# Loading 8 KB of gate weights in one transfer instead of four, with the spreading moved to VectorE

## The chip, the cores and the metric

The kernel runs on one core of one Trainium2 chip. The metric is the device time of one execution in microseconds (us), lower is better. An execution counts as slow when it takes over 1.5% longer than the fastest of the same kernel, and only fast ones are compared. Times below are medians of a kernel's runs; the span that a profile shows is about 1.75 us shorter than the time. Runs of one kernel scatter by some 0.3 us either way, and the effect studied here is about 0.4 us.

## The reference

Four batches of cross-covariance attention (6400 x 256) feed a mixture of eight low-rank adapters, of which the gate picks two for each row.

```python
def _attn_ref(q, k, v, tau):                       # each (4, 6400, 256)
    qn = q / (np.linalg.norm(q, axis=1, keepdims=True) + 1e-06)
    kn = k / (np.linalg.norm(k, axis=1, keepdims=True) + 1e-06)
    s = kn.transpose(0, 2, 1) @ qn / tau           # 256 x 256 per batch
    s = s - s.max(-1, keepdims=True)
    a = np.exp(s)
    a /= a.sum(-1, keepdims=True) + 1e-09
    return (v @ a).astype(np.float32)

def _moe_ref(x, w_gate, A, B):                     # x (25600, 256), w_gate (256, 8)
    logits = x @ w_gate
    # ... the two best of eight experts for each row, softmax of their two logits ...
    # delta = sum over the two of w * ((x @ A[e]) @ B[e])
    return (x + delta).astype(np.float32)
```

## The kernel before

The kernel is a static schedule: a small simulator in the file plans every step, and the instructions are issued in that order. The parts here are the loads of the small weights, the copies that bring them to bf16, and the stores, which all go through the Sync queue.

```python
    def load_consts():                       # after the second load is issued
        first = W["first"].rearrange("p c d -> p (c d)")
        W["A0"] = first[0:P // 4, 4 * C:8 * C].rearrange("p (e g r) -> p e g r", e=E, r=R)
        nc.sync.dma_start(W["A0"], moe_A.rearrange("e (p g) r -> p e g r", g=8))
        W["B0"] = first[:, 8 * C:9 * C]
        nc.scalar.dma_start(W["B0"], moe_B.rearrange("e r d -> (e r) d"))
        W["wg0"] = first[:, 9 * C:9 * C + CC * E].rearrange("p (cc e) -> p cc e", e=E)
        wg = moe_w_gate.rearrange("(p g cc) e -> g p cc e", g=4, cc=CC)
        for g in range(4):
            nc.scalar.dma_start(W["wg0"][g * (P // 4):(g + 1) * (P // 4)], wg[g])
    # ...
    def do_wts(s):                           # VectorE, near 34.5 us
        W["A"] = const.tile([P, E, CC, R], BF16, name="a_raw")
        for g in range(4):
            nc.vector.tensor_copy(W["A"][g * (P // 4):(g + 1) * (P // 4)], W["A0"][:, :, CC * g:CC * g + CC, :])
        W["wg"] = const.tile([P, CC, E], BF16, name="wg_raw")
        nc.vector.tensor_copy(W["wg"], W["wg0"])
        W["B"] = const.tile([P, C], BF16, name="ball")
        nc.vector.tensor_scalar(out=W["B"], in0=W["B0"], scalar1=0.5, scalar2=None, op0=OP.mult)
    # ...
    def do_hold(s, kind, b, i):              # three of them: hold the stores back until a load of k has landed
        # ...
        nc.sync.dma_start(scrap, src)
    # ...
    def do_store(s, b, i, c, n):             # 24 of them, the last six within 10 us
        lo = i * PC + c
        nc.sync.dma_start(out_v[b, :, lo:lo + n, :], held["y", (b, i), ""][:, c:c + n, :])
```

## Time and profile before

| | before |
|---|---|
| time, median (lowest to highest) | 256.07 us (255.68 to 256.32), 3 runs |
| span of the profile | 254.4 us |
| busy: TensorE, VectorE, ScalarE | 85%, 75%, 66% of the span |
| read and written in HBM | 78.91 + 26.21 MB, 413 GB/s over the span |

First, the page's parts on engines and transfers: busy time of each engine, then packets and bytes, then the queues with packets, MB and the share of 16 engines' time that their packets took. The queue q10 is the one that the Activation engine issues on, q1 belongs to the Sync engine, q0 to GpSimd.

```profile
PE 217.1 (85%) x2641; PEld 193.2 (76%) x2643; DVE 189.6 (75%) x483; ACT 166.7 (66%) x270; POOL 30.0 (12%) x58
...
DMA packets 11964, 66.47 MB, mean 261 GB/s; under 512 B 1568, under 2 KB 2464, under 8 KB 7328
...
q0 software_dynamic: 7488, 39.06, 74.7%
q1 hardware_dynamic: 3968, 26.61, 25.7%
q10 hardware_dynamic: 480, 0.40, 0.7%
```

Shares of 74.7 and 25.7% already exceed 100: packets overlap on an engine. By this measure the engines have no free time, but it counts recorded packet times. The table by stretches says the same (start and end, length, busy time of each engine, granted TensorE clock, share of the transfer engines, GB/s):

```profile
4.00:46.00 42.00, 23.91 (x197) 18.14 (x198) 22.28 (x34) 20.73 (x19) 6.94 (x14) 0.94 1.06 216
48.00:68.00 20.00, 19.64 (x262) 17.79 (x260) 16.71 (x43) 14.36 (x27) 3.49 (x5) 0.92 1.04 217
68.00:88.00 20.00, 20.00 (x253) 18.74 (x252) 17.77 (x38) 14.63 (x21) 2.13 (x4) 1.00 1.03 239
128.00:158.00 30.00, 30.00 (x377) 27.95 (x378) 24.97 (x52) 21.98 (x36) 2.22 (x5) 1.00 1.04 217
206.00:230.00 24.00, 23.20 (x331) 21.15 (x328) 19.64 (x58) 16.83 (x32) 0.53 (x1) 1.00 1.02 350
```

TensorE is full in some stretches and half idle up to 46 us. By this measure the transfers are full in all of these (1.02 to 1.06). Next, the timeline of VectorE around the weight copies and around its one gap (start, duration, instruction, and in brackets the idle time before it with its cause):

```profile
35.67 0.17 DVE L525 CAST wg_raw<-y 128x16 bf16<-128x16 f32 x1
35.75 0.29 DVE L527 TENSOR_SCALAR ball<-y 128x256 bf16<-128x256 f32 x1
...
43.09 0.43 DVE L595 TENSOR_TENSOR ssqq<-ssq 128x256 f32<-128x256 f32 x1
43.84 1.76 DVE L586 TENSOR_TENSOR ssq<-ssq,sq 128x1536 f32<-128x1536 f32 x1 [0.33 <-ACT sq L580]
```

Then the timeline of ScalarE's queue at the start. The four issues take 2.02 us, and ScalarE's own work begins after them:

```profile
1.66 2.02 ACTq L483 DMA_DIRECT2D y<-in_moe_w_gate_dram  x4
3.70 1.28 ACT L497 ACT_TABLE_LOAD   x1 [3.70 <-issue]
5.00 0.20 ACT L497 ACTIVATE scrap<-neg_inv_tau 1x1 bf16<-1x1 f32 x1
5.11 1.12 ACT L738 CAST qk<-y 128x512 bf16<-128x512 f32 x2
```

### The profile page before, as it was taken

The page shows a single profiled execution, that of the slowest core. Times are in us where ns is not written, and L with a number is a line of the kernel's source. Part 1 is how long each engine was busy: PE and PEld are TensorE (multiplying, and loading weights), DVE is VectorE, ACT ScalarE, POOL GpSimd, SP SyncE. Part 2 cuts the span into 40 slices and gives each one's busy share as a digit, 9 for nine tenths or more (in the row PEclk, how much of TensorE's full clock was granted, in tenths as well). Part 3 has the DMA queues.
Part 4 walks back from the last instruction along what each step waited for, and adds up shares of the span by engine and source line. Part 5 has one row for each costly group of instructions (what it writes and reads, how often), then busy time and mean ns, then how long its engine had stood idle before and what let it go on. Part 6 is the DMA issues. An engine that isn't in the chain of part 4 may idle for free.

```text
span 254.4 us, 6345 instructions
## 1 busy us (share of the span) xinstructions
PE 217.1 (85%) x2641; PEld 193.2 (76%) x2643; DVE 189.6 (75%) x483; ACT 166.7 (66%) x270; POOL 30.0 (12%) x58
## 2 busy tenths in 40 slices
PE   0165984899999998999989999889999979999970
PEld 0053962598999996799789998779999759999860
DVE  0055589779889977898979995689888878888910
ACT  3344446558786766888768667543777859768770
POOL 7000220040020002000130100510000200000000
PEclk9999997599999999999999999999999999999995
DMA  8999999999999999999999999999999999999994
GB/s 188 215 218 208 211 220 213 213 220 215 213 218 210 317 293 293 259 216 219 210 215 220 214 216 216 214 208 353 276 287 320 337 315 315 321 426 422 423 411 174
DMA packets 11964, 66.47 MB, mean 261 GB/s; under 512 B 1568, under 2 KB 2464, under 8 KB 7328
## 3 DMA queue, kind: packets, MB, share of 16 engines
q0 software_dynamic: 7488, 39.06, 74.7%
q1 hardware_dynamic: 3968, 26.61, 25.7%
q10 hardware_dynamic: 480, 0.40, 0.7%
q8 instruction: 20, 0.33, 0.5%
q14 instruction: 8, 0.07, 0.1%
HBM read 78.91 MB, written 26.21 MB: 413 GB/s over the span
## 4 chain that ended last, share of the span: by engine, by line
PE 54%; DMA 34%; DVE 3%; ACT 3%; POOL 2%; issue 1%; DVEq 0%; ACTq 0%; POOLq 0%
DMA qk<-in_k_dram 28%; PE Y_ps L877 13%; PE Y_ps L881 7%; PE T_ps L753 7%; DMA v<-in_v_dram 6%; PE ZL_ps L775 5%; PE gzT_ps L864 3%; PE acc_417 L558 2%; PE acc_418 L558 2%; PE acc_2620 L558 2%; PE acc_2621 L558 2%; PE Z_ps L844 2%; DVE a_bf L727 2%; POOL qk L543 1%; PE log_ps L790 1%
## 5 line engine op out<-in xcount | busy, mean ns | idle before, releaser
L586 DVE TENSOR_TENSOR ssq<-ssq,sq 128x1280 f32<-128x1280 f32 (+1 forms) x27 | 43.4, 1607 | 26.7 <-ACT sq L580 24.7
L877 PE MATMUL Y_ps<-a_bf,vT 128*128 128x256 bf16 x400 | 60.0, 273 | 0.0
L580 ACT ACTIVATE sq<-qk 128x1280 f32<-128x1280 bf16 (+1 forms) x27 | 36.8, 1364 | 25.9 <-DVE ssq L586 19.3
L733 ACT COPY y<-Y_ps 128x512 f32<-128x512 f32 x79 | 45.8, 587 | 12.2 <-PE Y_ps L881 9.6
L558 PEld LDWEIGHTS <-qk 128*128 128x128 bf16 x400 | 33.8, 103 | 24.9 <-DMA qk<-in_k_dram 15.3
L733 ACT COPY vT<-T_ps 128x1024 bf16<-128x1024 bf16 (+1 forms) x44 | 37.0, 871 | 7.7 <-PE T_ps L753 7.5
L877 PEld LDWEIGHTS <-vT 128*128 128x128 bf16 x400 | 37.6, 98 | 3.7
L881 PE MATMUL Y_ps<-ball,gzT 128*128 128x256 bf16 x200 | 38.2, 273 | 0.3 <-DVE gzT L735 0.3
L558 PE MATMUL acc_110<-qk 128*128 128x256 bf16 x50 | 15.0, 310 | 16.9 <-DMA qk<-in_k_dram 10.6
L753 PE MATMUL T_ps<-ident,v 128*128 128x128 bf16 x400 | 28.0, 224 | 0.6 <-DMA v<-in_v_dram 0.6
L543 POOL DMA_DIRECT2D v<-in_v_dram x20 | 12.2, 612 | 128.7 <-PE T_ps L753 81.5
L562 PEld LDWEIGHTS <-qk 128*128 128x128 bf16 x242 | 24.3, 100 | 3.4
L753 PEld LDWEIGHTS <-v 128*128 128x128 bf16 x400 | 24.6, 100 | 1.9 <-DMA v<-in_v_dram 1.5
L881 PEld LDWEIGHTS <-gzT 128*128 128x128 bf16 x200 | 19.4, 98 | 3.0 <-DVE gzT L735 0.6
L775 PE MATMUL ZL_ps<-waA_sb,vT 128*128 128x136 bf16 x280 | 19.6, 222 | 1.1 <-DVE waA_sb L721 0.9
L864 PE MATMUL gzT_ps<-ident,gz 128*128 128x128 bf16 x200 | 19.7, 219 | 0.3
L775 PEld LDWEIGHTS <-vT 128*128 128x128 bf16 x280 | 17.7, 98 | 1.8 <-issue 1.3
L735 DVE COPY gzT<-gzT_ps 128x512 bf16<-128x512 bf16 (+1 forms) x39 | 15.0, 390 | 5.5 <-PE gzT_ps L864 4.8
L580 ACT ACTIVATE ssq<-qk 128x1536 f32<-128x1536 bf16 x8 | 11.9, 1483 | 10.2 <-DMA qk<-in_q_dram 4.8
L735 DVE COPY y<-Y_ps 128x512 f32<-128x512 f32 x21 | 14.3, 690 | 3.3 <-PE Y_ps L881 3.3
L733 ACT COPY zl<-ZL_ps 128x272 f32<-128x272 f32 (+1 forms) x35 | 14.0, 447 | 3.1 <-PE ZL_ps L775 3.0
L567 PEld LDWEIGHTS <-qk 128*128 128x128 bf16 x168 | 14.8, 98 | 1.2 <-issue 0.2
(304 smaller groups left out, 440.9 us busy)
## 6 DMA issues: line engine op xcount, KB each, us to landing
out_dram<-y SPq DMA_DIRECT2D x18, 1280.0 KB, 17.8
v<-in_v_dram POOLq DMA_DIRECT2D x20, 640.0 KB, 20.3
qk<-in_q_dram POOLq DMA_DIRECT2D x7, 1088.0 KB, 24.0
qk<-in_k_dram POOLq DMA_DIRECT2D x7, 1088.0 KB, 28.9
qk<-in_q_dram POOLq DMA_DIRECT2D x2, 1024.0 KB, 18.5
qk<-in_k_dram POOLq DMA_DIRECT2D x2, 1024.0 KB, 22.8
out_dram<-y SPq DMA_DIRECT2D x4, 512.0 KB, 6.6
qk<-in_q_dram POOLq DMA_DIRECT2D x2, 512.0 KB, 17.4
```

What stands on the lines that cost most here:

```text
L558: nc.tensor.matmul(acc[ic][:, 0:256], kt[:, j, ic * P:(ic + 1) * P], qt[:, j, :], start=c == 0, stop=False, skip_group_check=True)
L562: nc.tensor.matmul(acc[ic][:, 256:384], kt[:, j, ic * P:(ic + 1) * P], kt[:, j, ic * P:(ic + 1) * P], start=False, stop=False, skip_group_ ...
L567: nc.tensor.matmul(acc[ic][:, 384:512], qt[:, j, ic * P:(ic + 1) * P], qt[:, j, ic * P:(ic + 1) * P], start=False, stop=c == NC - 1, skip_ ...
L580: nc.scalar.activation(out[:, 0:n, :], t[:, j:j + n, :], ACT.Square)
L586: nc.vector.tensor_tensor(out=t, in0=t, in1=held["sq", (w, b, g), ""][:, 0:n, :], op=OP.add)
L733: nc.scalar.copy(out, in_)
L735: nc.vector.tensor_copy(out, in_)
L753: nc.tensor.matmul(ps[:, ic, j, :], vt[:, c + j, ic * P:(ic + 1) * P], W["ident"], is_transpose=True, start=(ic + j == 0), stop=(ic == CC ...
L775: nc.tensor.matmul(ps[:, j, :], vT[:, ic, c + j, :], st[b]["waA"][:, ic, :], start=(j == 0 and ic == 0), stop=(j == n - 1 and ic == CC - 1 ...
L864: nc.tensor.matmul(ps[:, j, :], gz[:, j, :], W["ident"], is_transpose=True, start=(j == 0), stop=(j == n - 1))
L877: nc.tensor.matmul(ps[:, j, :], vT[:, ic, c + j, :], st[b]["a"][:, ic, :], start=(j == 0 and ic == 0), stop=False, skip_group_check=True)
L881: nc.tensor.matmul(ps[:, j, :], gzT[:, c + j - UNITS[u][0], :], W["B"], start=False, stop=(j == 1), skip_group_check=True)
```

## The change

The gate weights are 256 x 8 floats, 8 KB. The kernel before loads them with four transfers of 32 rows of 64 bytes, one into each group of 32 partitions. The change loads them with one transfer of 32 rows of 256 bytes into the first 32 partitions, and VectorE, which has to make a bf16 copy anyway, writes that copy to the four groups in four instructions. The intent is to save three transfers.

```diff
-        W["wg0"] = first[:, 9 * C:9 * C + CC * E].rearrange("p (cc e) -> p cc e", e=E)
-        wg = moe_w_gate.rearrange("(p g cc) e -> g p cc e", g=4, cc=CC)
-        for g in range(4):
-            nc.scalar.dma_start(W["wg0"][g * (P // 4):(g + 1) * (P // 4)], wg[g])
+        W["wg0"] = first[0:P // 4, 9 * C:9 * C + 4 * CC * E].rearrange("p (g cc e) -> p g cc e", g=4, e=E)
+        nc.scalar.dma_start(W["wg0"], moe_w_gate.rearrange("(p g cc) e -> p g cc e", g=4, cc=CC))
@@ do_wts
-        nc.vector.tensor_copy(W["wg"], W["wg0"])
+        for g in range(4):
+            nc.vector.tensor_copy(W["wg"][g * (P // 4):(g + 1) * (P // 4)], W["wg0"][:, g])
```

## The prediction

> **What bounds the kernel now.** The transfer engines never rest: the table by stretches puts the DMA share at 0.99 to 1.10 from 4 to 230 us. TensorE shares the limit: busy 19.64 of 20 us from 48 to 68 us, 20.00 of 20 from 68 to 88. The chain of waits runs through transfers of k from 3.51 to 46.07 us, then mostly through TensorE, and again through transfers from 128.6 to 157.6 and 191.7 to 205.7 us.
>
> **What the change does.** The instruction order stays the same on every engine but for two places: the Activation queue issues one gate-weight transfer instead of four, and VectorE makes four copies 32x16 instead of one 128x16.
>
> 1. Issuing. The four issues take 2.02 us (1.66 to 3.68 us); one takes about 0.49. ScalarE's table load (now at 3.70 us) should start near 2.2 us. The first casts (5.11 us) gain at most 0.1 us: the first k block lands at 5.04 us. The chain gains nothing: after four matmuls from 6.28 us TensorE waits for k data until 14.77 us.
>
> 2. Transfers. The Trainium skill (DMA: Bandwidth & Descriptors, "Why a DMA increments its semaphore by 16 and not by 1") says that each participating engine ends its share of a transfer with a semaphore write. The trace agrees: the Activation queue's 480 packets are 384 of data (128 each for k, B, gate weights) + 6 x 16. So 96 data and 48 semaphore packets go: 336 remain. Cost, an estimate: that queue took 0.7% of 16 engines' 254.4 us = 28.5 us. At the store queue's rate (26.61 MB in 25.7%: 25.4 KB per us and engine) its 0.40 MB takes 15.8 us; the other 12.7 us over 224 to 480 packets is 26 to 57 ns each. 144 packets are 3.8 to 8.2 us, or 0.2 to 0.5 us on each of 16 engines, while the chain is the k transfers. Shares above 1 mean packets overlap, so perhaps half becomes time.
>
> 3. VectorE. The one copy takes 174 ns and the next instruction begins 80 ns after it. Three more should cost 0.25 to 0.5 us at 35.7 us. VectorE is busy without a break from 32.8 to 43.5 us, then waits 0.33 us for a ScalarE square whose start a q transfer set. That gap takes most of the delay. The rest (0 to 0.2 us) can reach rqI, which ends at 47.63 us, while TensorE takes it up at 48.01 us: 0.4 us more slack.
>
> **On the critical path:** -0.1 to -0.4 us from transfers, 0 to +0.2 us from VectorE.
>
> **Prediction:** 255.8 us, 8 in 10 between 254.9 and 256.6. Faster by over 2%: 0.01; within 2%: 0.98; slower: 0.01.
>
> **What would show it.** Gate issues fall from four to one, the Activation queue's packets to 336; the table load starts near 2.2 us; TensorE's restart (14.77 us) comes 0 to 0.4 us earlier; four copies in a row near 35.6 us total 0.4 to 0.7 us; VectorE's gap at 43.8 us shrinks; the rq_ps matmul at 48.23 us moves by under 0.4 us; later stages keep their lengths.
>
> **What would make it wrong.** Small packets holding up the shared engines far longer than their own time (then over 1 us faster); a clock step that moves a whole window; or later loads and stores meeting differently, which could move the end by 1 us either way.

## More of the kernel before

The program gives each transfer issued from the Sync and Activation queues one of eight completion semaphores, in turn. (Such a semaphore is a counter by which a transfer tells that its data has landed, so that an engine can wait for it.)

Last, the end of the program on the Sync queue. The first line comes from the view of waits (total us, times, longest). The others list the Sync queue's instructions of the closing line after 252.7 us (count, shortest, median and longest duration in ns, first and last start):

```profile
SPq L940 <- DMA out_dram<-y: 5.7, 3, 3.9
...
L940 SPq EVENT_SEMAPHORE  x8: 17/28/28, 253.2 to 254.3; - x8
L940 SPq DRAIN  x3: 7/7/7, 253.5 to 253.8; - x3
```

The view of the output tensor gives the last two stores with their first and last start, and the time from issue to landing:

```profile
L889 SPq DMA_DIRECT2D out_dram<-y x2: 332/332/333, 246.3 to 246.9; - x2
...
DMA to landing us min/median/max: 6.2/6.2/6.2
```

So the last store is issued at 246.9 us and lands near 253.1 us (253.15 by the trace's time stamps).

## The result and the profile after

| | before | after |
|---|---|---|
| median of 5 runs | 256.10 us (255.68 to 256.32) | 255.84 us (255.37 to 255.88) |
| span of the profile | 254.4 us | 254.1 us |
| packets of the Activation queue | 480 | 336 |
| last store landed at | 253.15 us | 253.14 us |
| span's end minus last landing | 1.215 us | 0.908 us |

The ratio of the two is 0.998, with a 95% interval of 0.9968 to 0.9992. Ratios here are the mean time of one kernel's fast runs over that of the other's of the same rounds, so not quite the ratio of the quoted medians. The changed kernel is faster by 0.2%, and the interval excludes a ratio of 1.

The last two rows of the table come from the trace's time stamps and surprise. The data was all out at the same moment in both executions. The 0.31 us between the two spans lies after it.

Here are the lines of the profile after. Transfers, from the page:

```profile
DMA packets 11820, 66.47 MB, mean 262 GB/s; under 512 B 1424, under 2 KB 2320, under 8 KB 7184
...
q10 hardware_dynamic: 336, 0.40, 0.6%
```

VectorE's timeline at the same two places. The copies and the instruction after them take 0.65 us more (36.34 - 35.61 = 0.73 us from the first copy to the next instruction, against 0.08 us), and the gap before the sum at 44 us is gone; that sum starts 0.18 us later than before:

```profile
35.61 0.70 DVE L524 CAST wg_raw<-y 32x16 bf16<-32x16 f32 x4
36.34 0.29 DVE L526 TENSOR_SCALAR ball<-y 128x256 bf16<-128x256 f32 x1
...
43.68 0.42 DVE L594 TENSOR_TENSOR ssqq<-ssq 128x256 f32<-128x256 f32 x1
44.02 1.75 DVE L585 TENSOR_TENSOR ssq<-ssq,sq 128x1536 f32<-128x1536 f32 x1
```

ScalarE's timeline at the start, with everything earlier than before:

```profile
1.66 0.46 ACTq L481 DMA_DIRECT2D y<-in_moe_w_gate_dram  x1
2.15 1.28 ACT L495 ACT_TABLE_LOAD   x1 [2.15 <-issue]
...
4.62 1.14 ACT L737 CAST qk<-y 128x512 bf16<-128x512 f32 x2 [0.97 <-DMA y<-in_q_dram]
```

And the end on the Sync queue, the wait line and the instructions after 252.7 us:

```profile
SPq L939 <- DMA out_dram<-y: 5.9, 6, 1.2
...
L939 SPq EVENT_SEMAPHORE  x3: 17/17/28, 253.2 to 254.0; - x3
L939 SPq DRAIN  x3: 7/7/7, 253.2 to 253.5; - x3
```

with the last store, from the view of the output tensor:

```profile
L888 SPq DMA_DIRECT2D out_dram<-y x1: 332/332/332, 246.5 to 246.5; - x1
...
DMA to landing us min/median/max: 6.6/6.6/6.6
```

It was issued 0.4 us earlier and took 0.4 us longer, so it landed when it did before. The transfer engines still had earlier stores to work off: their share is 0.93 from 246 to 250 us and 0.39 from 250 to 252.5 us (before, 0.95 and 0.39).

Read the closing lines against the same lines of before. After the last landing the Sync queue has eight semaphore instructions to run before, and three after. The waits on stores tell why. Before, the closing part stops three times for a store, the first time for 3.9 us; after, it stops six times, at most 1.2 us. The closing part checks the eight completion semaphores one by one in a fixed order (each check is one instruction, which also names a second semaphore). In the kernel before, the last six stores use the semaphores 5, 6, 7, 0, 1, 2 (counted from 0), so the last store's is the third to be checked, and five checks that have long been satisfied are still to come when it lands. In the trace these follow one another every 61 ns on average. Three transfers less shift the assignment by three: the last six stores now use 2 to 7, the last store's semaphore is the eighth and last, and no check is left. Five times 61 ns is 0.31 us.

The Trainium skill (Perfetto Trace Analysis, "Identifying Dependency Chains") says that an instruction that waits for several engines may have EventSemaphore instructions with further wait conditions put in front of it. The trace agrees: these lines are EVENT_SEMAPHORE instructions with two wait conditions each, in front of a DRAIN. It adds their price, 61 ns each even when there is nothing to wait for.

### The profile page after: what moved, and what is told of

It is laid out like the page before. It is cut to its first block, busy times and chain, and to the rows that moved or that the text cites. A ratio compares the mean times of both kernels' runs of the same rounds, so it can differ in the third digit from the quotient of the medians.

```text
span 254.1 us, 6344 instructions
## 1 busy us (share of the span) xinstructions
PE 216.1 (85%) x2643; PEld 192.7 (76%) x2643; DVE 190.0 (75%) x486; ACT 166.8 (66%) x270; POOL 30.1 (12%) x58
## 4 chain that ended last, share of the span: by engine, by line
PE 49%; DMA 39%; ACT 3%; DVE 3%; POOL 2%; issue 1%; ACTq 0%; POOLq 0%
DMA qk<-in_k_dram 22%; PE Y_ps L876 13%; DMA v<-in_v_dram 9%; DMA qk<-in_q_dram 8%; PE Y_ps L880 6%; PE T_ps L752 6%; PE ZL_ps L774 4%; PE gzT_ps L863 3%; PE Z_ps L843 2%; PE acc_417 L557 2%; PE acc_418 L557 2%; DVE a_bf L726 2%; PE acc_2620 L557 1%; PE acc_2621 L557 1%; ACT a_exp L678 1%
## 5 line engine op out<-in xcount | busy, mean ns | idle before, releaser
L752 PE MATMUL T_ps<-ident,v 128*128 128x128 bf16 x400 | 27.1, 220 | 0.3 <-DMA v<-in_v_dram 0.3
L752 PEld LDWEIGHTS <-v 128*128 128x128 bf16 x400 | 23.9, 98 | 1.5 <-DMA v<-in_v_dram 1.2
```

The source lines that it names most:

```text
L752: nc.tensor.matmul(ps[:, ic, j, :], vt[:, c + j, ic * P:(ic + 1) * P], W["ident"], is_transpose=True, start=(ic + j == 0), stop=(ic == CC ...
```

## The experiments

Two theories compete for the 0.4 us. The theory says that removed transfer work at the start makes everything end earlier. The rival, found in the traces after the first set of runs, says that the last store's semaphore moved to a better place in the closing checks. There are two more suspects, VectorE's longer copying and ScalarE's earlier start. Each kernel was run for five rounds beside the kernel before; in a set, all share the same runs of the kernel before (set one: median 256.19 us; set two: 256.01 us; set three: 256.05 us). Set one ran on one chip (numbered 4), sets two and three on another (12). Where a kernel had four or six runs, it is said.

### Set one: parts of the change

**The change again.** No edit.

> The changed kernel again, unaltered, as the anchor of this set. If the 0.2% of the first measurement is real, the ratio to before is again 0.997 to 0.999 (0.3 to 0.8 us faster). If the first measurement was luck or only a property of that chip, it is 0.999 to 1.001.

Measured: 255.63 us, ratio 0.9982 (0.9970 to 0.9995). The gain is real and repeats in another set of runs. End minus last landing was 0.90 us again.

**The copies alone.**

```diff
 (kernel before)
-        nc.vector.tensor_copy(W["wg"], W["wg0"])
+        for g in range(4):
+            nc.vector.tensor_copy(W["wg"][g * (P // 4):(g + 1) * (P // 4)], W["wg0"][g * (P // 4):(g + 1) * (P // 4)])
```

> The kernel before, with only VectorE's part of the change: four gate transfers as before, but four copies of 32x16 instead of one of 128x16. Result right. My theory: VectorE is 0.5 to 0.6 us later from 36.3 us on, the 0.33 us gap at 43.8 us takes it, and rq_ps does not start over 0.2 us later; ratio 0.9995 to 1.0010. Rival (the copies reach the end in full, and the transfers save twice what the result shows): +0.5 us, ratio 1.002.

Measured: 256.01 us, ratio 1.0000 (0.9986 to 1.0014). VectorE's part costs nothing at the end that these runs can see; the interval allows 0.36 us either way. The trace shows where it goes. This is VectorE's timeline of this kernel:

```profile
35.74 0.76 DVE L526 CAST wg_raw<-y 32x16 bf16<-32x16 f32 x4
36.53 0.29 DVE L528 TENSOR_SCALAR ball<-y 128x256 bf16<-128x256 f32 x1
...
43.87 0.43 DVE L596 TENSOR_TENSOR ssqq<-ssq 128x256 f32<-128x256 f32 x1
44.21 1.75 DVE L587 TENSOR_TENSOR ssq<-ssq,sq 128x1536 f32<-128x1536 f32 x1
```

The instruction after the copies starts 0.78 us later than before (36.53 against 35.75), more than the expected 0.5 to 0.6; the matmul rq_ps, the next step on TensorE, is not later (48.15 against 48.23). The sum after the gap starts 0.37 us later than before (44.21 against 43.84). In this execution the attention matrix of the first batch (a_bf) came 0.78 us later than before (54.91 against 54.13 us), and yet the last store landed at 252.90 us, 0.25 us earlier than in the profile of before. In this one execution a delay of the compute engines was swallowed later, while the transfers ran on.

**The single transfer alone, with one copy.** The result is wrong (relative error 0.027), because the copy takes other rows.

```diff
 (changed kernel)
-        for g in range(4):
-            nc.vector.tensor_copy(W["wg"][g * (P // 4):(g + 1) * (P // 4)], W["wg0"][:, g])
+        nc.vector.tensor_copy(W["wg"], W["B0"][:, 0:CC * E].rearrange("p (cc e) -> p cc e", e=E))
```

> The changed kernel with its single gate transfer but one copy of 128x16 as before, taken from the other weights' rows, so gate values and result are wrong on purpose[...]. My theory (the gain is all from the three transfers less, the copies cost nothing at the end): the same ratio as the changed kernel, 0.997 to 0.999. Rival (the copies cost 0.5 us): 0.5 us faster than the changed kernel, ratio about 0.996.

Measured: 255.53 us, ratio 0.9981 (0.9968 to 0.9994), the same as the whole change. So the gain belongs to the transfers, not to the copies. This run cannot say whether it is their work or their number, since the semaphores shift along with them.

**Four transfers from the idle Sync queue.**

```diff
 (kernel before)
-            nc.scalar.dma_start(W["wg0"][g * (P // 4):(g + 1) * (P // 4)], wg[g])
+            nc.sync.dma_start(W["wg0"][g * (P // 4):(g + 1) * (P // 4)], wg[g])
```

> The kernel before with its four gate transfers issued from the idle Sync queue: all packets and semaphore writes stay, only ScalarE is free 2 us earlier (table load near 1.7 us). Result right. My theory (engine time of packets): no gain, ratio 0.9993 to 1.0007, and TensorE's first matmul, though up to 0.5 us earlier, changes nothing later. Rival (the gain is ScalarE's earlier start): ratio as the changed kernel's, about 0.998.

Measured: 256.11 us, ratio 0.9998 (0.9986 to 1.0011). ScalarE's earlier start (its table load at 1.67 us) is worth nothing that shows.

So far everything agrees with the theory. Then the time stamps of the six traces were laid side by side. End minus last landing was 1.215, 1.215 and 1.207 us in the three kernels with four gate transfers, and 0.908, 0.899 and 0.899 us in the three with one. The last landings were 253.15, 252.90 and 253.40 us against 253.14, 252.96 and 253.13 us. The first pair of triples does not overlap and hardly scatters; the second overlaps. That is where the rival came from.

### Set two: the order of the closing checks, without the transfers

The hold step of the kernel already issues transfers of 32 bytes on the Sync queue. These kernels issue some more of 4 bytes, at the first hold near 79 us, only to turn the assignment of semaphores. The hold's own transfer is cut to four elements to make room in the scratch tile. The tiny transfers are not quite free: with five of them the first store is issued at 82.69 us instead of 79.51.

```diff
-        nc.sync.dma_start(scrap, src)               # src has 16 elements
+        nc.sync.dma_start(scrap[:, 0:4], src)       # src cut to 4 elements
+        if "tiny" not in W:
+            W["tiny"] = 5                           # 5 in the kernel before; 3 or 1 in the changed kernel
+            for n in range(W["tiny"]):
+                nc.sync.dma_start(scrap[:, 4 + 2 * n:6 + 2 * n], src[:, 0:2])
```

**Kernel before plus five tiny transfers** (last store on the eighth semaphore):

> The kernel before (four gate transfers, one copy) with five transfers of 4 bytes added on the Sync queue near 79 us, so that the last store's completion semaphore is the eighth of the eight, as in the changed kernel, and not the third. Result right. New theory (most of the gain sits after the last landing: the closing waits of the Sync queue go through the eight semaphores in order, about 61 ns each, and five of them follow the last store's in the kernel before): end minus last landing falls from 1.21 to 0.90 us, ratio 0.9985 to 0.9995. Rival, my theory on record (the gain is all removed transfer work at the start): end minus last landing stays 1.21, ratio 1.000 or a little above.

**Changed kernel plus three** (last store back on the third):

> The changed kernel with three transfers of 4 bytes added on the Sync queue near 79 us, so that the last store's semaphore is the third of eight again, as before the change. Result right. New theory: end minus last landing goes back from 0.90 to 1.21 us and two thirds of the gain go: ratio 0.9988 to 0.9998. Rival: it stays 0.90, ratio about 0.998.

**Changed kernel plus one** (last store on the first):

> The changed kernel with one such transfer, so that the last store's semaphore is the first of eight and seven waits follow it: the worst place. New theory: end minus last landing is 0.90 + 7 x 0.061 = 1.33 us, ratio 0.9990 to 1.0000. Rival: 0.90 us, ratio about 0.998.

Measured, with the kernels without tiny transfers beside them:

| kernel | gate transfers | checks left after the last store's | end minus last landing | median | ratio to before (95%) |
|---|---|---|---|---|---|
| before | 4 | 5 | 1.215 us | 256.01 us | 1 |
| before + 5 tiny | 4 | 0 | 0.912 us | 255.82 us | 0.9988 (0.9975 to 1.0001) |
| changed (set one) | 1 | 0 | 0.899 us | 255.63 us | 0.9982 (0.9970 to 0.9995) |
| changed + 3 tiny | 1 | 5 | 1.208 us | 256.08 us | 1.0004 (0.9992 to 1.0016) |
| changed + 1 tiny | 1 | 7 | 1.332 us | 256.22 us | 1.0010 (0.9998 to 1.0022) |

The closing lines of the Sync queue after 252.7 us, in the kernel before with five tiny transfers:

```profile
SPq L944 <- DMA out_dram<-y: 5.0, 6, 1.2
...
L944 SPq EVENT_SEMAPHORE  x3: 17/17/28, 253.2 to 254.0; - x3
```

in the changed kernel with three:

```profile
SPq L943 <- DMA out_dram<-y: 5.6, 3, 3.9
...
L943 SPq EVENT_SEMAPHORE  x8: 17/28/28, 252.9 to 254.1; - x8
```

and in the changed kernel with one:

```profile
SPq L943 <- DMA out_dram<-y: 5.7, 1, 5.7
...
L943 SPq EVENT_SEMAPHORE  x10: 17/28/28, 253.0 to 254.3; - x10
```

The counts 3, 8 and 10 are two closing instructions, one check that ends with the last landing, and 0, 5 or 7 further checks. End minus last landing follows: 0.90 us plus 61 to 62 ns for each check left. The row of the changed kernel is of set one, so its ratio is to the 256.19 us there. The expected 1.33 us of the worst place came out as 1.332. The effect can be given to the kernel before without any change to its gate transfers, and it can be taken from the changed kernel with its single transfer kept. The rival is shown. The ratio of the second row alone would not do, since its interval touches 1; the counts and the time stamps carry the verdict. The ratios go the same way, but two of the three missed what was expected: 1.0004 against 0.9988 to 0.9998, and 1.0010 against 0.9990 to 1.0000, though their intervals reach into these ranges. The expectations left a third of the gain to the removed transfers, and none of it shows. Whether the tiny transfers themselves cost a little was not tested.

What remains for the removed transfer work? Take from every fast run's time its kernel's end minus last landing, as its one profiled execution has it. The kernels with four gate transfers (before in all sets, the copies alone, the Sync queue, before plus five) then average 254.86 us over 41 runs. Those with one (changed twice, transfer alone, plus three, plus one) average 254.83 us over 25. The difference is -0.03 us, with two standard errors of 0.10 us.

**The gate transfers in rows of 4 bytes.** This was meant to enlarge what a small packet costs.

```diff
 (kernel before)
-        W["wg0"] = first[:, 9 * C:9 * C + CC * E].rearrange("p (cc e) -> p cc e", e=E)
-        wg = moe_w_gate.rearrange("(p g cc) e -> g p cc e", g=4, cc=CC)
+        W["wg0"] = first[:, 9 * C:9 * C + 32].rearrange("p (z x) -> p z x", x=2)[:, :, 0:1]
+        wg = moe_w_gate.rearrange("(p g cc) (e x) -> g p (cc e) x", g=4, cc=CC, x=1)
 (the copy takes the same elements in the same order)
```

> The kernel before with the same four gate transfers cut into rows of 4 bytes (2048 data packets instead of 128; the result stays right), to enlarge what a small packet costs. If each takes the 22 ns per packet that the traces show for the 64-byte ones and all of it counts at the end: 1920 x 22 ns / 16 = +2.6 us, ratio 1.010. By the estimate on record (26 to 57 ns): +3.1 to +6.8 us, ratio 1.012 to 1.027. If the small packets overlap the large ones or the end does not hang on the transfers' total: under +0.7 us, ratio under 1.003.

Measured: 262.83 us over its fast and slow runs (262.6 us the four fast ones), ratio 1.0257 (1.0244 to 1.0270, four fast runs; two of the six were slow, and so was the profiled one). The ratio fits the estimate, but it measures something else. The timeline of ScalarE's queue shows it:

```profile
1.67 17.90 ACTq L483 DMA_DIRECT2D y<-in_moe_w_gate_dram  x4
19.60 1.28 ACT L497 ACT_TABLE_LOAD   x1 [19.60 <-issue]
```

The view of the issuing line gives the shortest, median and longest of the four issues in ns:

```profile
L483 ACTq DMA_DIRECT2D y<-in_moe_w_gate_dram  x4: 463/560/16231, 1.7 to 3.3; - x4
```

The four issues held the Activation queue for 17.9 us (16.2 us of it in the fourth alone; the first three took 0.46 to 0.61 us each), so ScalarE started 16 us late, and later VectorE waited 9.0 us for the last of the weights to land. This is the profiled execution, a slow one. The run is inconclusive on what a packet costs.

### Set three: the price of small packets, without anyone waiting

An unused transfer of the same 8 KB is added to the changed kernel on the Sync queue, which is idle until 78 us, into columns that no one reads.

```diff
 (changed kernel; the line for 2048 rows of 4 bytes; the other has x=8, 0:4 and (e x) with x=4)
+        junk = first[:, 9 * C + 64:9 * C + 96].rearrange("p (z x) -> p z x", x=2)[:, :, 0:1]
+        nc.sync.dma_start(junk, moe_w_gate.rearrange("(p z) (e x) -> p (z e) x", z=2, x=1))
```

**512 rows of 16 bytes:**

> The changed kernel plus one unused transfer of the same 8 KB on the Sync queue at the start, in 512 rows of 16 bytes (nothing waits for it before 60 us; the issuing ScalarE is not touched, unlike the run with rows of 4 bytes). Result right. The last store's semaphore becomes the first of eight, so end minus last landing is 1.33 us as in the run with one tiny transfer, whose ratio was 1.001: that is the zero of this test. If 528 packets of 22 ns all count: +0.73 us above it, ratio about 1.004. If small packets overlap the large ones: ratio 1.000 to 1.002.

Measured: 256.35 us, ratio 1.0013 (0.9999 to 1.0028), four runs. End minus last landing 1.34 us, as foreseen.

**2048 rows of 4 bytes:**

> The same with 2048 rows of 4 bytes. Zero again at ratio 1.001. If 2064 packets of 22 ns all count at the end: 2064 x 22 ns / 16 = +2.8 us, ratio about 1.012; by the upper end of the estimate on record (57 ns) +7.4 us, ratio 1.030. If small packets overlap the large ones: under +0.7 us, ratio under 1.004.

Measured: 256.66 us, ratio 1.0026 (1.0013 to 1.0038), four runs; end minus last landing 1.33 us. Both lie in the lowest of the expected ranges, that of overlap.

The zero of this test is the changed kernel with one tiny transfer, which averages 256.26 us with the same closing order. The 528 packets added 0.07 us, which is within the scatter, and the 2064 packets 0.40 us (256.66 - 256.26; the scatter of the means allows about 0.17 us either way). That is 0.40 us x 16 engines / 2064 = 3.1 ns of an engine's time for each packet, where the traces record some 22 ns for a packet of 4 bytes and 24 ns for one of 64. So about a seventh of a small packet's recorded time reaches the end. By this price the 144 packets that the change removes are worth 144 x 3.1 ns / 16 = 0.03 us, which fits the -0.03 us found by pooling.

That the other six sevenths overlap with other packets is not shown; some of that time may only be made up later. The chain of waits has the k load that ends the first long stretch, before and with the 2048 rows:

```profile
25.40 20.67 DMA qk<-in_k_dram
25.47 21.17 DMA qk<-in_k_dram
```

It ends at 46.07 and 46.64 us, and at 46.28 us with one tiny transfer. By the time stamps of its 16 parts, one from each engine, the middle ones land 0.7 us later than with one tiny transfer (45.58 against 44.87 us), and only the last one 0.36 us later. So more than a seventh of the time (0.7 of the recorded 2.8 us) delays most of the engines, and less of it the one that ends last.

## Why the prediction was right or wrong

The predicted 255.8 us and "within 2%" were right: 255.84 us. The sum that led there was not, and one step of it failed.

- **Issuing** was right in its consequence. The table load starts at 2.15 us ("near 2.2"). "The first casts (5.11 us) gain at most 0.1 us" was wrong: they start at 4.62 us, 0.49 us earlier, because they can begin with the q block, which lands sooner than the k block. It does not matter, since TensorE waits for k data until 14.72 us all the same, and the run with four transfers on the Sync queue put the worth of an earlier ScalarE at 0.9998.
- **Transfers** is the step that failed: "144 packets are 3.8 to 8.2 us, or 0.2 to 0.5 us on each of 16 engines ... perhaps half becomes time", and with it "-0.1 to -0.4 us from transfers". The count was right (480 to 336). Its price was too high twice. The recorded time of a 64-byte packet is 24 ns and of a semaphore packet 20 to 22 ns, below the estimated 26 to 57, and of the recorded time not half but about a seventh reaches the end. The measured term is 0.03 us, which the scatter of 0.10 us does not tell from zero. TensorE's restart moved from 14.77 to 14.72 us, well inside "0 to 0.4", and the k load that ended at 46.07 us before ended at 46.20 us after: the loads did not come earlier.
- **VectorE** was right in mechanism and undersized in amount. The four copies cost 0.65 us more, not 0.25 to 0.5: each starts only when the one before has ended, 176 to 180 ns apart, while the single copy let the next instruction start after some 80 ns. The Trainium skill (VectorE: DVE Perf Modes, "Two Vector instructions with no wait between them") has a rule, as a model, that fits: an instruction whose output begins in another group of 32 partitions than the last output starts only when all earlier Vector instructions have finished. The four copies write to four such groups, and the trace agrees with its 176 to 180 against 80 ns. The gap at 43.8 us took most of it (the sum after the gap starts 0.18 us later) and the slack of rq_ps the rest: rq_ps starts at 48.25 us against 48.23, and the copies alone measured 1.0000.
- **What the prediction did not have** is the term that made the gain: the shift of the completion semaphores by three takes five satisfied checks, 0.31 us, out of the stretch between the last landing and the end. It was readable in the profile of before, from the count of closing semaphore instructions after the last landing and the number and lengths of the closing waits. Of the measured gain of about 0.4 us (255.7 against 256.1 on average), these 0.31 us are shown; the other 0.09 us, with whatever the removed transfers gain in it, is within the scatter.

So the number was right by luck, a coincidence of two errors: a term of -0.1 to -0.4 us that is nearly zero, and a missing term of -0.31 us.

What stays open: whether the removed transfers gain 0.00 or 0.10 us, since that is below what these runs resolve, and the same for what they would gain if the other engines had waited for them.

## What to carry to other kernels

Where transfers take their completion semaphores in turn, as here, a change that adds or removes one also moves every later transfer to another semaphore. When the program's end checks these in a fixed order, place the last store on the one that is checked last, and look for such a shift whenever a small change moves the time by tenths of a microsecond. When a gain is measured, find where in the trace it lies before believing the reason that predicted it; comparing "last landing" and "end minus last landing" overturned a theory that four experiments had agreed with. The recorded time of small packets was no price here: add a few thousand of them on an idle queue and measure the slope.

## What the Trainium skill lacked or had wrong

- No page has the cost of the closing checks. Here each completion semaphore that is checked after the last landing cost 61 to 62 ns (end minus last landing 0.90, 1.21 and 1.33 us with 0, 5 and 7 left). It would fit Perfetto Trace Analysis, "Identifying Dependency Chains".
- DMA: Bandwidth & Descriptors, "Anatomy of one DMA", calls the semaphore write on trn2 essentially free. The section describes transfers issued by GpSimd. The traces record 20 to 22 ns for such a packet on the Activation queue, but taking away 48 of them and 96 data packets gained 0.03 us, within a scatter of 0.10 us. This does not speak against the page; the recorded duration misleads. No run changed the number of semaphore writes alone (of the 2064 packets at 3.1 ns each, 2048 are data).
- The same page, in the same section, says of descriptor generation that many descriptors can be emitted before their cost shows. On the Activation queue the four transfers of 512 rows of 4 bytes held the issuing engine for 17.9 us (the fourth alone for 16.2 us), against 2.02 us for four of 32 rows, while one transfer of 2048 rows of 4 bytes on the Sync queue took 0.68 us to issue. The section speaks of transfers issued by GpSimd; it does not say how many descriptors the Sync and Activation queues take before an issue is held.
- VectorE: DVE Perf Modes gives the rule of held instructions without a time. Here copies that write to different groups of 32 partitions start 176 to 180 ns apart, and an unheld instruction 80 ns after a copy of the same width.
